# Attention and two expert layers in one kernel: the values' products of two tiles together every second step, x's transposes in front of them, values converted three steps sooner

## The chip, the cores and the metric

One core of a Trainium2 chip runs one launch. The time is device microseconds; the median of three runs of the kernel before is 1000.96 us (998.5 to 1001.49). The profiled execution, from which every duration below comes, took 1003.76 us, of which 1002.0 us lie between the first and the last instruction.

## The reference

Three stages follow each other. The first is causal attention with a position bias for 4 batches, 8 heads, 576 positions and 64 columns per head:

```
s_pos = maximum(s, 0);  cum = cumsum(s_pos, -1)
scores = q @ k.T / 8 + minimum(-(cum_i - cum_j), 0), causal
attn = exp(scores - max) / (sum + 1e-9)
x = (attn @ v), heads side by side: [2304, 512]
```

The second is `relu(x @ w_in)**2 @ w_out` (512 to 2048 to 512), the third `g = h * cos(h)` with `h = x @ w_in`, then `g @ w_out`, with weights of its own. Everything is float32.

## The kernel before

Precision comes from splitting a number into a high and a low part and adding three products (high*high, low*high, high*low). The first expert layer does this in a 32-bit type for TensorE (`F32R`), attention's values and the second expert layer in float16.

The 2304 tokens form nine blocks of 256. Attention's work is cut into 160 jobs: a job is one head (of one of 12 stretches of queries) times one tile of up to 128 queries. The 32 jobs of the first 16 heads (`EARLY`) are computed from float32 values, the other 128 ("late") from split float16 values. A job passes through a pipeline, one stage per step of the main loop, and `step` (called for every step) writes the instructions of all engines in its order: scores (`emit_qk`, line 496, TensorE, into one of three PSUM buffers), mask and row maximum (`emit_mask`, line 510, VectorE), exponentials (`emit_exp`, line 527, ScalarE), the split into two float16 parts and the transposition of both by a DMA on SyncE's queue (`emit_split`, lines 555 to 565, from tile `p` to tile `pt`, three buffers), and the products with the values (`emit_pv`, line 590, TensorE, 3 products for every 128 keys, 64 columns each, into `pvs`). Job j's products stand at the end of step j+5 (`LAG`). When the two heads of a pair are through (every four jobs where heads have two tiles, every two where they have one), `evacuate` (lines 618 to 630, VectorE) divides by the sums in the next step and writes `xp`; `turn` (line 644, TensorE) transposes it through the identity into `xps` at the end of that step, after the products; `x_high` and `x_low` (lines 655, 661) split it in the step behind.

Between these stand the products of the first expert layer for the block that attention has finished: `g1` (line 844, 12 products, called G1 below) and `g2` (line 873, 12 products, G2). A step has one to two such slots: first slot, scores, second slot, the values' products, transposes.

The values are prepared in 16 groups of two heads, on a list `vq` from which every step takes one entry at its end (`v_late`): load (GpSimd queue, line 379), squares (`v_square`, ScalarE, line 390), their sum over partitions by a product with ones (`v_sum`, line 398, TensorE, into another part of `xps`), a power of two from it (`v_scale`, VectorE, lines 404 and 409), high and low part, and the store to `v_d`, from which `load_v` reads per head. `v_steps` puts the groups on steps: `V_TIME` says how long before its first use a group is due.

After the last attention block the second expert layer (lines 1230, 1285) runs from about 620 us to the end.

Of the kernel before, what the change touches and what calls it, by code (L numbers as in the profile page):

```python
# [8 lines left out]
F32 = mybir.dt.float32  # L9
# [81 lines left out]

KQ = 832

WAHEAD = 8
# [15 lines left out]
V_NEAR = 6  # L110
V_TIME = 7


@with_exitstack
def attention_moe_moe_kernel(
# [44 lines left out]

    ones = const.tile([128, 128], F32, name="ones")
    yss = const.tile([128, 2 * NB1], F32, name="yss")
# [41 lines left out]
    def load_sums(x, eng):  # L204
        nc_ = c8[2 * x:2 * x + 2, 0:BT]
        eng.dma_start(out=early[x][64:65, :, BT:2 * BT], in_=nc_)
        eng.dma_start(out=early[x][65:66, :, 0:BT], in_=nc_)

    def load_raw(n):
        nq, nl = heads[n][6], heads[n][8]  # L210
        if n < H:
            return
        if n < EARLY:
            t = at.tile([128, KQ], F32, tag=("hi", "k2")[n % 2], bufs=2, name="early1")
            nc.sync.dma_start(out=t[0:64, 0:2 * BT], in_=qk[n, 0:64, 0:2 * BT])
            nc.sync.dma_start(out=t[64:66, 0:2 * BT], in_=c1_d[n - H])
            hd[n] = t
            return
        raw = at.tile([128, KQ], F32, tag="raw", bufs=2, name="raw")
        nc.sync.dma_start(out=raw[:, BT - nq:BT + nl], in_=qk[n, :, BT - nq:BT + nl])  # L220
        hd[n] = [None, None, raw]
# [111 lines left out]
    def load_ext(n):  # L333
        nq, nl = heads[n][6], heads[n][8]
        if n < EARLY:
            return
        hd[n][0] = at.tile([128, KQ], F32R, tag="hi", bufs=2, name="hi")
        hd[n][1] = at.tile([128, KQ], F32R, tag="k2", bufs=2, name="k2")
        nc.gpsimd.dma_start(out=hd[n][1][64:68, BT - nq:BT + nl], in_=ext_d[n, :, BT - nq:BT + nl])  # L339

    def prep_high(n):
        nq, nk = heads[n][6], heads[n][8]
        if n < EARLY:
            return
        hi, k2, raw = hd[n]
        nc.scalar.copy(hi[:, BT - nq:BT + nk], raw[:, BT - nq:BT + nk])
        nc.scalar.copy(k2[0:64, BT - nq:BT], raw[0:64, BT - nq:BT])

    def prep_low(n):
        nq, nk = heads[n][6], heads[n][8]  # L350
        if n < EARLY:
            return
        hi, k2, raw = hd[n]
        nc.vector.tensor_tensor(
            out=hi[64:128, BT - nq:BT], in0=raw[64:128, BT - nq:BT], in1=hi[64:128, BT - nq:BT], op=ALU.subtract
        )
        nc.vector.tensor_tensor(  # L357
            out=k2[0:64, BT:BT + nk], in0=raw[0:64, BT:BT + nk], in1=hi[0:64, BT:BT + nk], op=ALU.subtract
        )
# [35 lines left out]
    def v_sum(g):  # L395
        n = g[2]
        vs[g]["ps"] = xps[:, BT:BT + n]
        nc.tensor.matmul(vs[g]["ps"], ones, vs[g]["ss"])

# [48 lines left out]
    def v_steps(gs, start):  # L448

        at, due = [], len(jobs) + V_TIME  # L450
        for b, h, n, nch in reversed(gs):
            first = next(
                i for i, j in enumerate(jobs) if j[0] >= 2 * H and heads[j[0]][1] == b and h <= heads[j[0]][2] < h + n
            )
            due = min(first - start + 3 - V_TIME, due - V_NEAR)
            at.insert(0, due)
        free = 0
        for x, due in enumerate(at):
            at[x] = max(0, min(due, free))
            free = at[x] + V_STRIDE  # L460
        return at

    def v_add(gs, at, stored=True):

        for g, t in zip(gs, at):
            fs = []
            if g not in vs:
                fs, t = [(t, v_load)], t + 2
            fs += [(t, v_square), (t + 1, v_sum), (t + 2, v_scale), (t + 2, v_high), (t + 3, v_low)]
            for x, f in fs + [(t + 3, v_store)] * stored:  # L470
                vq.extend([] for _ in range(x + 1 - len(vq)))
                vq[x].append((f, g))
# [3 lines left out]
    def emit_qk(i):  # L476
# [5 lines left out]
        segs = [(0, 288), (288, 288)] if w > 512 else [(0, max(w, 256))]  # L482
        qo = BT - nq + q - q0
        if n < EARLY:
# [7 lines left out]
        for k, (c0, cn) in enumerate(segs):  # L492
            p = psa.tile([128, 512], F32, tag=f"qk{flip[0]}", bufs=1, name="qkp")
            flip[0] = (flip[0] + 1) % 3
            for m, kk in ((hi, 128), (k2, 68)):
                nc.tensor.matmul(  # L496
                    p[0:r, 0:cn], m[0:kk, qo:qo + r], m[0:kk, BT + c0:BT + c0 + cn],
                    start=(kk == 128), stop=(kk == 68),
                )
# [40 lines left out]
    def emit_split(i):  # L540
# [21 lines left out]
        )  # L562
        pt = at.tile([128, 1280], F16, tag="pt", bufs=3, name="pt")
        pt = pt[:, 0:2 * cw // 128 * r].rearrange("p (a r) -> p a r", r=r)
# [112 lines left out]
    def lag(i):  # L677
        return LAG[not job(i) or jobs[i][0] >= EARLY]

# [5 lines left out]
    def unit_done(u):  # L685
        return last_job[u] + lag(last_job[u]) + 3

# [295 lines left out]
    def step(moe=0, bits=0, attn=True):  # L983

        i = prog[0]
        prog[0] += attn
        if attn:
            for j in stage(1, i - 2):
# [32 lines left out]
        if attn:  # L1021
            for j in stage(0, i - 2):
                if jobs[j][1] == 0:
                    load_v(jobs[j][0])
            for j in stage(3, i - LAG[0]):
                if j > i - lag(j):
                    stages[3] -= 1
                    break
                emit_pv(j)
        turn()  # L1030
        w_ahead()
# [375 lines left out]
```

## Time and profile before

| | before |
|---|---|
| median of 3 runs | 1000.96 us |
| profiled execution | 1003.76 us |
| its span | 1002.0 us |
| TensorE busy in the span | 966.9 us (96%) |
| VectorE busy | 723.9 us (72%) |
| ScalarE busy | 655.5 us (65%) |
| mean granted TensorE clock | 0.995 |

TensorE's matmuls are pipelined, so what a group costs is read from the start of its first to the start of what follows, not from the lengths of the rows. In a window's row the columns after the stretch are the busy time of PE (matmuls), PEld (weight loads), VectorE, ScalarE and GpSimd with the number of instructions, then the granted clock, the DMA engines' share and GB/s. In a timeline row the columns are start, length, engine, line, operation, written tile `<-` read tiles, shape, count, and in brackets the idle time before and what ended it.

### The profile page before, as it was taken

The page shows a single profiled execution, that of the slowest core. Times are in us where ns is not written, and L with a number is a line of the kernel's source. Part 1 is how long each engine was busy: PE and PEld are TensorE (multiplying, and loading weights), DVE is VectorE, ACT ScalarE, POOL GpSimd, SP SyncE. Part 2 cuts the span into 40 slices and gives each one's busy share as a digit, 9 for nine tenths or more (in the row PEclk, how much of TensorE's full clock was granted, in tenths as well). Part 3 has the DMA queues.
Part 4 walks back from the last instruction along what each step waited for, and adds up shares of the span by engine and source line. Part 5 has one row for each costly group of instructions (what it writes and reads, how often), then busy time and mean ns, then how long its engine had stood idle before and what let it go on. Part 6 is the DMA issues. An engine that isn't in the chain of part 4 may idle for free.

```text
span 1002.0 us, 20487 instructions
## 1 busy us (share of the span) xinstructions
PE 966.9 (96%) x7266; PEld 740.6 (74%) x7266; DVE 723.9 (72%) x1865; ACT 655.5 (65%) x1596; POOL 163.2 (16%) x258
## 2 busy tenths in 40 slices
PE   5999899999999999999999999999999999999998
PEld 4788898899999998999999997444544454444444
DVE  6879788867777897787888267798887545555555
ACT  4789777767777777767776578777766444433433
POOL 2000011111111121111211023330033341000000
PEclk9999999999999999999999999999999999999999
DMA  8955599746887986467898569210000000011001
GB/s 268 292 182 181 118 202 203 170 111 157 196 162 160 178 193 175 109 155 145 192 206 180 188 237 360 95 43 1 1 1 1 0 1 1 0 43 43 23 20 64
DMA packets 150711, 126.65 MB, mean 126 GB/s; under 512 B 108048, under 2 KB 125792, under 8 KB 150608
## 3 DMA queue, kind: packets, MB, share of 16 engines
q1 hardware_dynamic: 146688, 119.05, 46.1%
q0 software_dynamic: 3904, 6.29, 2.5%
q8 instruction: 57, 0.93, 0.4%
q14 instruction: 46, 0.38, 0.1%
q10 hardware_dynamic: 16, 0.01, 0.0%
HBM read 85.25 MB, written 15.81 MB: 101 GB/s over the span
## 4 chain that ended last, share of the span: by engine, by line
PE 79%; DVE 8%; DMA 6%; ACT 4%; issue 2%; SPq 1%; DVEq 0%; ACTq 0%
PE hps L844 18%; PE y L873 18%; PE o L1285 17%; PE hp L1230 17%; PE qkp L496 4%; PE pvs L590 4%; DMA rw<-in_w_dram 3%; DMA raw<-in_qk_dram 1%; PE xps L644 1%; DVE st L716 1%; DVE sb L510 1%; DVE gl L863 1%; DVE wt L737 0%; DVE k L357 0%; SPq L178 0%
## 5 line engine op out<-in xcount | busy, mean ns | idle before, releaser
L844 PE MATMUL hps<-xh,wt 128*128 128x256 f32 x1152 | 241.4, 292 | 4.1 <-ACT g L855 4.0
L873 PE MATMUL y<-gh,wt 128*128 128x256 f32 x1152 | 237.7, 289 | 0.0
L844 PEld LDWEIGHTS hps<-xh,wt 128*128 128x128 f32 x1152 | 191.7, 194 | 7.0 <-ACT g L855 5.5
L873 PEld LDWEIGHTS y<-gh,wt 128*128 128x128 f32 x1152 | 189.9, 192 | 1.3
L1230 PE MATMUL hp<-yh,wt 128*128 128x512 f16 (+1 forms) x640 | 185.9, 358 | 0.0
L1285 PE MATMUL o<-wt,gh 128*128 128x512 f16 x576 | 171.3, 379 | 2.0 <-ACT wt L1300 1.9
L873 PE MATMUL y<-gl,wt 128*128 128x256 f32 x576 | 163.4, 284 | 2.6 <-DVE gl L863 2.6
L844 PE MATMUL hps<-xl,wt 128*128 128x256 f32 x576 | 164.3, 285 | 0.9 <-DVE xl L661 0.9
L1230 PEld LDWEIGHTS <-wt 128*128 128x128 f16 x960 | 92.2, 98 | 93.3
L1242 ACT ACTIVATE a<-hp,hsc 128x512 f32<-128x512 f32 (+1 forms) x80 | 51.4, 643 | 118.6 <-PE hp L1230 117.2
L855 ACT ACTIVATE g<-hps 128x256 f32<-128x256 f32 x144 | 54.6, 379 | 107.7 <-PE hps L844 105.8
L1230 PE MATMUL hp<-yl,wt 128*128 128x512 f16 (+1 forms) x320 | 114.4, 358 | 0.0
L873 PEld LDWEIGHTS y<-gl,wt 128*128 128x128 f32 x576 | 110.6, 192 | 3.7 <-DVE gl L863 3.1
L844 PEld LDWEIGHTS hps<-xl,wt 128*128 128x128 f32 x576 | 111.7, 194 | 1.4 <-DVE xl L661 1.1
L1285 PE MATMUL o<-wt,gl 128*128 128x512 f16 x288 | 109.2, 379 | 0.4 <-DVE gl L1272 0.4
L1243 DVE TENSOR_SCALAR kf<-a 128x512 f32<-128x512 f32 (+1 forms) x80 | 34.5, 431 | 103.8 <-ACT a L1242 103.4
L1285 PEld LDWEIGHTS <-gh 128*128 128x128 f16 x576 | 56.2, 98 | 66.7 <-issue 2.4
L527 ACT ACTIVATE sb<-sb,nb 128x128 f32<-128x128 f32 (+8 forms) x160 | 93.7, 586 | 12.1 <-DVE nb L510 12.0
L339 POOL DMA_DIRECT2D k<-ext_d x80 | 40.8, 510 | 341.9 <-ACT g L856 92.3
L510 DVE CUSTOM_DVE_ANT_0 sb<-qkp,mask 128x128 f32<-128x128 f32 (+8 forms) x160 | 72.7, 454 | 13.8 <-PE qkp L487 8.6
L1251 ACT ACTIVATE a<-kf 128x512 f32<-128x512 f32 (+1 forms) x80 | 46.8, 585 | 46.6 <-DVE kf L1244 46.1
L559 DVE SCALAR_TENSOR_TENSOR p<-sb,p 128x512 f16<-128x512 f32 (+7 forms) x128 | 72.4, 565 | 4.0
(119 smaller groups left out, 1680.1 us busy)
## 6 DMA issues: line engine op xcount, KB each, us to landing
rw<-in_w_dram SPq DMA_DIRECT2D x64, 512.0 KB
raw<-in_qk_dram SPq DMA_DIRECT2D x32, 352.0 KB
raw<-in_qk_dram SPq DMA_DIRECT2D x16, 384.0 KB
v_d<-vt SPq DMA_DIRECT2D x16, 320.0 KB
raw<-in_qk_dram SPq DMA_DIRECT2D x16, 320.0 KB
vb<-v_d SPq DMA_DIRECT2D x32, 160.0 KB
vr<-in_v_dram POOLq DMA_DIRECT2D x15, 320.0 KB, 4.7
y_d<-yst SPq DMA_DIRECT2D x18, 256.0 KB
```

Source lines behind the costliest of these rows:

```text
L339: nc.gpsimd.dma_start(out=hd[n][1][64:68, BT - nq:BT + nl], in_=ext_d[n, :, BT - nq:BT + nl])
L496: nc.tensor.matmul(p[0:r, 0:cn], m[0:kk, qo:qo + r], m[0:kk, BT + c0:BT + c0 + cn], start=(kk == 128), stop=(kk == 68),)
L510: nc.vector.tensor_tensor_reduce(out=sb[0:r, c0:c0 + cn], in0=p[0:r, 0:cn], in1=mask[0:r, mo + c0:mo + c0 + cn], scale=-0.125, scalar=(3.0 ...
L527: nc.scalar.activation(out=sb[0:r, 0:w], in_=sb[0:r, 0:w], func=ACTF.Exp, scale=-1.0, bias=j["nb"], accum_out=pd[n - h % 2]["z"][0:r, ti, ...
L559: nc.vector.scalar_tensor_tensor(out=p[0:r, cw:cw + w], in0=sb[0:r, 0:w], scalar=PSC, in1=p[0:r, 0:w], op0=ALU.mult, op1=ALU.subtract,)
L844: nc.tensor.matmul(hp, w[:, a, c * 128:(c + 1) * 128], (xh, xl)[e][:, c, :], start=(n == 0), stop=(n == 3 * KD - 1),)
L855: nc.scalar.activation(out=g, in_=hp, func=ACTF.Relu)
L873: nc.tensor.matmul(yps[k][d // 2][:, d % 2, :], w[:, a, d * 128:(d + 1) * 128], (gh, gl)[e], start=(f == 0 and n == 0 and d % 2 == 0), sto ...
L1230: nc.tensor.matmul(hp, w[:, a, c * 128:(c + 1) * 128], (yh, yl)[e][:, c, :], start=(m == 0), stop=(m == 3 * KD - 1),)
L1242: nc.scalar.activation(out=a, in_=hp, func=ACTF.Copy, scale=sm["hsc"][:, j, f:f + 1], bias=0.25)
L1251: nc.scalar.activation(out=a, in_=kf, func=ACTF.Sin, scale=-6.2831850)
L1285: nc.tensor.matmul(ops[j][a], (gh, gl)[e][:, a * 128:(a + 1) * 128], w[:, x, :], start=(first and m == 0), stop=(last and m == 2),)
```

## The change

Late jobs of odd number have a lag of 4 steps instead of 5, so that jobs 2m and 2m+1 both have their products at the end of step 2m+5, and the steps between have none. In a step with late products `turn` is called in front of them; in a step without, it is held back to the next. `pt` gets a fourth buffer for every fourth job (`pt4`, or `vt`'s space where the tile is largest); the space comes from narrower rows (`SQ` 768 instead of 832, with the place of the queries' start computed by `qb`) and from a `ones` of one column that is read as if it were 128. The groups of values start on even entries of `vq`, `V_TIME` is 10 instead of 7, and the sum comes two entries after the squares instead of one, with what follows one entry later too.

```diff
@@ -90,6 +90,7 @@
 KQ = 832
+SQ = 768
-V_TIME = 7
+V_TIME = 10
...
-    ones = const.tile([128, 128], F32, name="ones")
+    ones = const.tile([128, 1], F32, name="ones")
...
+    def qb(n):
+        return min(BT, SQ - heads[n][8])
...
-        raw = at.tile([128, KQ], F32, tag="raw", bufs=2, name="raw")
-        nc.sync.dma_start(out=raw[:, BT - nq:BT + nl], in_=qk[n, :, BT - nq:BT + nl])
+        raw = at.tile([128, SQ], F32, tag="raw", bufs=2, name="raw")
+        nc.sync.dma_start(out=raw[:, qb(n) - nq:qb(n) + nl], in_=qk[n, :, BT - nq:BT + nl])
...
-        nc.tensor.matmul(vs[g]["ps"], ones, vs[g]["ss"])
+        nc.tensor.matmul(vs[g]["ps"], ones.to_broadcast([128, 128]), vs[g]["ss"])
...
-            at[x] = max(0, min(due, free))
+            at[x] = max(0, min(due, free)) // 2 * 2
...
-            fs += [(t, v_square), (t + 1, v_sum), (t + 2, v_scale), (t + 2, v_high), (t + 3, v_low)]
-            for x, f in fs + [(t + 3, v_store)] * stored:
+            fs += [(t, v_square), (t + 2, v_sum), (t + 3, v_scale), (t + 3, v_high), (t + 4, v_low)]
+            for x, f in fs + [(t + 4, v_store)] * stored:
...
-        pt = at.tile([128, 1280], F16, tag="pt", bufs=3, name="pt")
+        if i % 4 < 3:
+            pt = at.tile([128, 1280], F16, tag="pt", bufs=3, name="pt")
+        elif cw * r <= 512 * 128:
+            pt = at.tile([128, 1024], F16, tag="pt4", bufs=1, name="pt4")
+        else:
+            pt = at.tile([128, 1280], F16, tag="vt", bufs=1, name="pt5")
...
     def lag(i):
-        return LAG[not job(i) or jobs[i][0] >= EARLY]
+        if job(i) and jobs[i][0] < EARLY:
+            return LAG[0]
+        return LAG[1] - (i % 2 if job(i) else 0)
...
-        return last_job[u] + lag(last_job[u]) + 3
+        return last_job[u] + lag(last_job[u]) + (4 if u > 1 else 3)
...
+        hold = False
...
+            js = []
             for j in stage(3, i - LAG[0]):
                 if j > i - lag(j):
                     stages[3] -= 1
                     break
+                js.append(j)
+            if js and jobs[js[0]][0] >= EARLY:
+                turn()
+            for j in js:
                 emit_pv(j)
-        turn()
+            if not js and job(i - 4) and jobs[i - 4][0] >= EARLY:
+                hold = True
+        if not hold:
+            turn()
```

Three places in the order of the instructions show what moves. On TensorE, in the third block (tiles of 128 and 64 queries), the kernel before has the products of the second tile (64x64), a G1, the scores of the next pair, the first tile's products and the transposes of the pair that went before, then a G2:

```order
L873 MATMUL y_2910<-gh,wt 128x256
L590 LDWEIGHTS pt
L590 MATMUL pvs<-vb,pt 64x64
...
L844 MATMUL hps<-xh,wt 128x256
...
L496 MATMUL qkp<-hi 128x448
L496 MATMUL qkp<-k_3489 128x448
L590 LDWEIGHTS pt
L590 MATMUL pvs<-vb,pt 128x64
...
L644 MATMUL xps<-ident,xp 128x128
L644 MATMUL xps<-ident,xp 128x64
L873 MATMUL y_2909<-gh,wt 128x256
```

The same place with the change, where lines 855 and 884 are G1 and G2, 500 the scores, 653 the transposes, 599 the values' products and 402 the sum with ones:

```order
L855 MATMUL hps<-xh,wt 128x256
L500 MATMUL qkp<-hi 128x448
L500 MATMUL qkp<-k_3497 128x448
L653 MATMUL xps<-ident,xp 128x128
L653 MATMUL xps<-ident,xp 128x64
L599 LDWEIGHTS pt
L599 MATMUL pvs<-vb,pt 128x64
...
L599 LDWEIGHTS pt
L599 MATMUL pvs<-vb,pt 64x64
...
L402 MATMUL xps<-ss,ones 128x2
L884 MATMUL y_2935<-gh,wt 128x256
```

The transposes stand between the scores and the products, both tiles' products (3 and 6 here) stand together, and one of the sums stands behind them; between G1 and the scores there are no products any more.

On VectorE, around the same pair's evacuation (z is the tile of the sums, `sb` the masked scores, `p` the split), before:

```order
L357 TENSOR_TENSOR k2_3568<-raw_3431,hi_3567 64x448
L618 SCALAR_TENSOR_TENSOR z_3228<-z_3228,vsc_89 128x2
...
L630 SCALAR_TENSOR_TENSOR xp_3638<-pvs_78,z_3228 128x128
L630 SCALAR_TENSOR_TENSOR xp_3638<-pvs_78,z_3228 64x128
L510 ISA sb_3645,nb_3646<-qkp_3600,mask_86 128x320
...
L555 TENSOR_SCALAR p_3648<-sb_3584 64x192
```

and with the change (line 639 evacuates, 514 masks, 559 splits):

```order
L874 TENSOR_TENSOR gl_3560<-g_3524,gh_3525 128x256
L627 SCALAR_TENSOR_TENSOR z_3248<-z_3248,vsc_89 128x2
...
L639 SCALAR_TENSOR_TENSOR xp_3596<-pvs_78,z_3248 128x128
L639 SCALAR_TENSOR_TENSOR xp_3596<-pvs_78,z_3248 64x128
L514 ISA sb_3603,nb_3604<-qkp_3562,mask_86 64x192
...
L514 ISA sb_3651,nb_3652<-qkp_3619,mask_86 128x320
```

The evacuation stands one job sooner: in front of the mask of a pair's last tile (64x192) instead of the mask of the next pair's first (128x320).

On TensorE the sum with ones (line 398, with the change 402) stood behind products or transposes in every late group; before, in the second block:

```order
L496 MATMUL qkp<-k_1450 128x512
L590 LDWEIGHTS pt
L590 MATMUL pvs<-vb,pt 128x64
...
L873 MATMUL y_1627<-gh,wt 128x256
L873 MATMUL y_1627<-gl,wt 128x256
```

and the sum of that block with the change:

```order
L855 MATMUL hps<-xl,wt 128x256
L855 MATMUL hps<-xh,wt 128x256
L402 MATMUL xps<-ss,ones 128x2
L884 MATMUL y_1644<-gh,wt 128x256
L884 MATMUL y_1644<-gl,wt 128x256
```

Seven of the late groups' sums stand like this one, alone between G1, G2 or scores; the others stand behind products or transposes.

## Rows read from the trace of the kernel before

**Rows 1.** Windows: four stretches, columns as told above.

```profile
110.00:200.00 90.00, 82.91 (x785) 77.29 (x786) 74.39 (x210) 65.43 (x179) 12.87 (x28) 0.96 0.81 178
200.00:480.00 280.00, 278.65 (x2713) 265.54 (x2711) 214.14 (x687) 206.52 (x581) 41.93 (x112) 1.00 0.71 159
480.00:560.00 80.00, 78.03 (x851) 76.48 (x850) 64.35 (x187) 53.87 (x138) 10.02 (x30) 1.00 0.81 176
620.00:1002.00 382.00, 375.24 (x1853) 178.72 (x1851) 247.00 (x453) 198.84 (x370) 75.95 (x58) 1.00 0.08 29
```

**Rows 2.** Timeline of TensorE, one step of the fourth block.

```profile
300.46 0.29 PE L844 MATMUL hps<-xh,wt 128*128 128x256 f32 x1
...
301.90 0.43 PE L590 MATMUL pvs<-vb,pt 128*128 128x64 f16 x9
302.17 0.36 PE L873 MATMUL y<-gh,wt 128*128 128x256 f32 x1
...
303.69 0.34 PE L496 MATMUL qkp<-hi 128*128 128x384 f32 x1
```

**Rows 3.** The same around transposes of x behind products.

```profile
309.52 0.42 PE L644 MATMUL xps<-ident,xp 128*128 128x128 f32 x2
309.69 0.36 PE L873 MATMUL y<-gh,wt 128*128 128x256 f32 x1
309.89 0.28 PE L873 MATMUL y<-gl,wt 128*128 128x256 f32 x1
```

**Rows 4.** The same where transposes stood behind a G1.

```profile
109.97 0.44 PE L644 MATMUL xps<-ident,xp 128*128 128x128 f32 x2 [0.38 <-DVE xp L630]
110.17 0.36 PE L873 MATMUL y<-gh,wt 128*128 128x256 f32 x1
```

**Rows 5.** Transpositions by DMA: line 565's instructions, nanoseconds least, median, most.

```profile
L565 SPq DMA_TRANSPOSE pt<-p x128: 1167/1225/2385, 107.1 to 549.6; - x128
```

**Rows 6.** Waits of TensorE from 110 to 560 us: total, times, longest.

```profile
PE hps L844 <- ACT g L855: 3.2, 4, 1.4
PE pvs L590 <- DVE xp L630: 2.5, 2, 1.4
PE xps L398 <- ACT vt L390: 1.5, 1, 1.5
```

**Rows 7.** Timeline: the two longest of these waits, and VectorE before the second.

```profile
117.74 0.38 PE L398 MATMUL xps<-ss,ones 128*128 128x2 f32 x2 [1.55 <-ACT vt L390]
...
194.25 0.68 DVE L881 COPY yst<-y 128x512 f32<-128x512 f32 x1
195.22 0.28 DVE L630 SCALAR_TENSOR_TENSOR xp<-pvs,z 64x128 f32<-64x128 f32 x1
...
195.55 0.63 PE L590 MATMUL pvs<-vb,pt 128*64 128x64 f16 x15 [1.39 <-DVE xp L630]
```

**Rows 8.** Windows: two stretches at half clock.

```profile
118.10:121.50 3.40, 3.40 (x16) 3.21 (x16) 1.22 (x4) 0.66 (x2) 0.00 (x0) 0.50 0.10 38
196.60:200.00 3.40, 3.40 (x18) 3.40 (x18) 2.53 (x11) 1.70 (x6) 0.37 (x1) 0.51 1.49 303
```

**Rows 9.** Timeline of TensorE around a sum with ones.

```profile
204.35 0.38 PE L398 MATMUL xps<-ss,ones 128*128 128x2 f32 x2
204.59 0.36 PE L873 MATMUL y<-gh,wt 128*128 128x256 f32 x1
```

**Rows 10.** Waits of SyncE's queue from 110 to 560 us.

```profile
SPq L565 <- PE pvs L590: 81.5, 71, 3.9
```

**Rows 11.** Timeline: transpositions' issues, and fillings of `p` that waited for one.

```profile
193.24 1.33 SPq L565 DMA_TRANSPOSE pt<-p  x1
...
197.62 0.37 POOL L554 MEMSET p<- 64x128 f16 x1 [2.44 <-DMA pt<-p]
...
535.65 1.34 SPq L565 DMA_TRANSPOSE pt<-p  x1
...
540.00 0.21 POOL L554 MEMSET p<- 128x128 f16 x1 [4.63 <-DMA pt<-p]
```

**Rows 12.** Timeline: a split's end, and the products two steps on.

```profile
435.38 0.62 DVE L559 SCALAR_TENSOR_TENSOR p<-sb,p 128x448 f16<-128x448 f32 x1
...
440.77 0.44 PE L590 MATMUL pvs<-vb,pt 128*128 128x64 f16 x9
```

**Rows 13.** The page's DMA issues: KB each, median us to landing.

```profile
vr<-in_v_dram POOLq DMA_DIRECT2D x15, 320.0 KB, 4.7
```

More of the change, by code (lines that the diff above doesn't have):

```diff
@@ L213, in load_raw @@
         if n < EARLY:
-            t = at.tile([128, KQ], F32, tag=("hi", "k2")[n % 2], bufs=2, name="early1")
+            t = at.tile([128, SQ], F32, tag=("hi", "k2")[n % 2], bufs=2, name="early1")
             nc.sync.dma_start(out=t[0:64, 0:2 * BT], in_=qk[n, 0:64, 0:2 * BT])
@@ L336, in load_ext @@
             return
-        hd[n][0] = at.tile([128, KQ], F32R, tag="hi", bufs=2, name="hi")
-        hd[n][1] = at.tile([128, KQ], F32R, tag="k2", bufs=2, name="k2")
-        nc.gpsimd.dma_start(out=hd[n][1][64:68, BT - nq:BT + nl], in_=ext_d[n, :, BT - nq:BT + nl])
+        hd[n][0] = at.tile([128, SQ], F32R, tag="hi", bufs=2, name="hi")
+        hd[n][1] = at.tile([128, SQ], F32R, tag="k2", bufs=2, name="k2")
+        nc.gpsimd.dma_start(out=hd[n][1][64:68, qb(n) - nq:qb(n) + nl], in_=ext_d[n, :, BT - nq:BT + nl])
     def prep_high(n):
@@ L345, in prep_high @@
         hi, k2, raw = hd[n]
-        nc.scalar.copy(hi[:, BT - nq:BT + nk], raw[:, BT - nq:BT + nk])
-        nc.scalar.copy(k2[0:64, BT - nq:BT], raw[0:64, BT - nq:BT])
+        nc.scalar.copy(hi[:, qb(n) - nq:qb(n) + nk], raw[:, qb(n) - nq:qb(n) + nk])
+        nc.scalar.copy(k2[0:64, qb(n) - nq:qb(n)], raw[0:64, qb(n) - nq:qb(n)])
     def prep_low(n):
@@ L354, in prep_low @@
         nc.vector.tensor_tensor(
-            out=hi[64:128, BT - nq:BT], in0=raw[64:128, BT - nq:BT], in1=hi[64:128, BT - nq:BT], op=ALU.subtract
+            out=hi[64:128, qb(n) - nq:qb(n)], in0=raw[64:128, qb(n) - nq:qb(n)], in1=hi[64:128, qb(n) - nq:qb(n)], op=ALU.subtract
         )
         nc.vector.tensor_tensor(
-            out=k2[0:64, BT:BT + nk], in0=raw[0:64, BT:BT + nk], in1=hi[0:64, BT:BT + nk], op=ALU.subtract
+            out=k2[0:64, qb(n):qb(n) + nk], in0=raw[0:64, qb(n):qb(n) + nk], in1=hi[0:64, qb(n):qb(n) + nk], op=ALU.subtract
         )
@@ L482, in emit_qk @@
         segs = [(0, 288), (288, 288)] if w > 512 else [(0, max(w, 256))]
-        qo = BT - nq + q - q0
+        qo = qb(n) - nq + q - q0
         if n < EARLY:
@@ L496, in emit_qk @@
                 nc.tensor.matmul(
-                    p[0:r, 0:cn], m[0:kk, qo:qo + r], m[0:kk, BT + c0:BT + c0 + cn],
+                    p[0:r, 0:cn], m[0:kk, qo:qo + r], m[0:kk, qb(n) + c0:qb(n) + c0 + cn],
                     start=(kk == 128), stop=(kk == 68),
```

## The prediction

> **What bounds the kernel now.** I read the windows first. From 200 to 480 us TensorE is busy for 278.7 of 280 us, and from 480 to 560 for 78.0 of 80; from 110 to 200 it misses 7 of 90, and the clock there is 0.96 [rows 1]. VectorE, the next engine, is at 83, 76 and 80% in the three stretches [rows 1]: the largest load beside TensorE, but not the bound. So in the stretch that the change touches, time goes only where TensorE needs less of it: fewer or cheaper instructions, or fewer waits. The timeline of TensorE comes next, for what an instruction costs in its place: the reader is to compare starts, not lengths. Then the waits of TensorE, with the few that are long [rows 6, 7], the clock behind them [rows 8], and last the transpositions, whose latency could make the shorter lag a new wait [rows 10 to 12].
>
> **Products in pairs.** The late jobs are the 128 that have a transposition by DMA [rows 5]; their products now stand in 64 places instead of 128. The products themselves stay. What goes is the change of kind: a G1 without products in front takes from 300.46 to 301.90, 1.44 us; a G2 behind products takes from 302.17 to 303.69, 1.52 us [rows 2]. So 0.08 us per place, and 64 places less: **-5.1 us**. It lies on TensorE, which waits for nothing there, so all of it counts. A change of kind that costs more at tiles of 64 queries would raise it; no row here bounds that, and I leave it out.
>
> **Transposes in front.** Two transposes behind products take from 309.52 to 309.69, 0.17 us, and the G2's first product then still takes 0.20 (to 309.89) [rows 3]. The change of kind back to G1 or G2 is counted above, once per pair of jobs. In front of the products the two cost at least the columns: 256 columns take a twelfth of 1.44 us, 0.12 [rows 2]; the nearest row is two transposes behind a G1 after a short wait, 0.20 us (109.97 to 110.17) [rows 4]. So between 0.05 us less and 0.03 more at each of 40 pairs of heads (80 late heads), -2.0 to +1.2 us; I take the middle, **-0.4**.
> The Trainium skill (TensorE: Matmul & The Clock Gate, LDWEIGHTS) gives a load of stationary values as columns over 1.2 GHz, an estimate of 0.107 us for 128 of them, and lets the next load run beside the present matmul. By that rule the second transpose of a pair waits for its own load wherever the two stand, so the move is worth only what the first one gains, and the sum would be the same within half a microsecond; no run here shows it apart.
>
> **Waits that the new order takes away.** TensorE waited 2.5 us for evacuations in two places [rows 6]: at 195.55 a pair's first products started 0.05 us after the evacuation that stood in the same step in front of them ended (195.22 plus 0.28) [rows 7]. With the change the evacuation stands a job sooner, and the next products a step later than it: a step is G1, products, G2 and scores, 300.46 to 303.69 and the scores, some 3.6 us [rows 2], and the waits were 1.4 us at most [rows 6]. **-2.5.** The one wait for the squares of the values, 1.5 us at 117.74 [rows 6, 7], goes because the sum stands two entries behind the squares instead of one: **-1.5.** About half a microsecond behind the end of each of these two longest waits the granted clock falls to 0.50, the lower of the two levels, for 3.4 us (118.1 and 196.6) [rows 8]; at half speed 3.4 us do the work of 1.7. Without the waits I take both falls as gone, **-3.4**; if waits elsewhere bring them back, 0.
>
> **SyncE's queue.** Transpositions stood at its head for 81.5 us because their buffer was still to be read by products of that step [rows 10]. With four buffers and the products of 4m, 4m+1 at step 4m+5, 4m+2 and 4m+3 at 4m+7, every buffer is read a step before its next writing, so the transposition goes when the split is done, and the loads of values, scores' rows and the first layer's stores behind it go sooner. Of the 3.2 us that TensorE waited for ScalarE's g [rows 6] a part is late rows of this queue: between 0 and -3.2, I take **-0.8**, since the loads' transfers take as long as before.
>
> **What it adds.** Seven late sums with ones stand alone between other products, so each has a change of kind of its own: the sum takes 0.24 us either way (204.35 to 204.59) [rows 9], the change 0.08: **+0.6.** Values: load, squares, sum, parts and store now span six entries and the next group's load stands on the entry of the last group's low part, whose input buffer it overwrites; the load waits on GpSimd for VectorE, with rows of the scores and fillings of `p` behind it. It lands 4.7 us after its issue [rows 13], and the squares come two steps later, 7.2 us in long steps: hidden; in the blocks with 24 jobs for the same 32 slots a step is some 2.7 us, two are 5.4, and a late load holds ScalarE and through it G2. Bounds 0 to +3. Waits that the uneven steps make (3.3 us without products, 3.9 with) are in no row: 0, if VectorE at 76 to 83% follows, and at most as many as stand there now, 4.0 us of the above [rows 6]. For both together I take the half of that, **+2.0.**
>
> **The sum.** -5.1 - 0.4 - 2.5 - 1.5 - 3.4 - 0.8 + 0.6 + 2.0 = -11.1 us. The profiled execution took 1003.76 us (1.76 of it around the span), which gives 992.7; it is 2.8 us above the median of the runs shown, 1000.96. What the second expert layer does behind 620 us is unchanged and starts earlier by the same amount. From the median: **990.0 us**. With the small terms at their ends (falls of the clock stay, +3.4; transposes +1.6 or -1.6; SyncE +0.8 or -2.4; new waits +3.0 or -2.0) added as independent errors, 985 to 995.
>
> **Rivals.**
> *Only the change of kind.* The waits of rows 6 and 7 come back a few steps on, since they come from ScalarE and VectorE being late at the ends of blocks, and the clock falls with them. For it: waits at such places have several causes [rows 6]. Against it: two of them hang on an order that is gone. -5.1 - 0.4 + 0.6 is -4.9: 996.
> *VectorE becomes the bound.* In the stretches at 80 and 83% [rows 1], 170 us long, the steps without products are 0.3 us shorter than the mean, and VectorE has a third of a microsecond less for its share; if TensorE then waits for what it gains there, nothing is left of the gain in 170 of 450 us, and the old waits, which lie there, stay. About two thirds of 4.9 are left: 998. Against it: VectorE's idle time is 17 to 24%, and a backlog of 0.3 us has the next step to be worked off.
> *Slower: the odd tile's products wait for its transposition.* They now come at the end of the second step after the split, where the even ones have three. In the shortest steps a split ends at 436.00, and products stand at 440.77: 4.8 us [rows 12]. Nearly always less is needed: a filling of `p` waited for a transposition issued at 193.24 and began at 197.62, so 4.4 us were enough [rows 11]. From 4.8 us on, each of the 24 pairs in the two blocks of short steps waits for the difference, and everything on TensorE behind it; at 5.3 us the gain of 11 is spent (24 times 0.5 is 12), at 5.6 it is 24 times 0.8, 19 us, and the time is 1009. For it: transpositions now run beside the loads that they used to come after. Against it: 4.4 us was one of the long ones, after a queue of loads, and the transpositions are issued earlier after the split than before.
> *More goes.* If the other waits of 110 to 200 us (7 us of TensorE idle [rows 1]) go too, 982.
>
> **How the numbers follow.** The forecast 0.62, only the change of kind 0.18, VectorE 0.11, slower 0.05, more 0.04. About 0.3%, 3 us, is what a measurement of this kernel can tell from no change. The forecast and "more" are faster; of the change-of-kind case nine tenths; of VectorE's case a third: faster 0.86, the same 0.09, slower 0.05. The range takes the forecast's own 985 to 995, the first rival, and part of the others: 984 to 997.
>
> **What would show it.** Right: 64 groups of products where 128 were; a G1 or G2 behind none of them at 1.44 us; no wait of SyncE's transpositions for products; no wait of products for an evacuation, nor of the sum for squares; no fall of the clock near 118 and 196 us; attention's end, the last transposition by DMA, some 11 us earlier. Wrong: products that wait with no engine named, which would be transpositions; waits for VectorE's masks, gl or splits of more than 4 us together; or a clock at half speed at new places.

## The result: slower, and the profile after

| | before | after |
|---|---|---|
| median of 6 runs | 1001.01 us (998.5 to 1003.16) | 1009.81 us (1008.06 to 1011.76) |
| ratio | | 1.009 [1.007, 1.011] |
| profiled execution | 1003.76 us | 1008.63 us |
| its span | 1002.0 us | 1006.8 us |
| TensorE busy | 966.9 us | 961.2 us |
| mean granted TensorE clock | 0.995 | 0.989 |

The forecast was 990.0 us, so it missed by 20 us and on the wrong side. TensorE is busy 5.7 us less than before, as was meant; it stands idle longer. Line numbers from here on are those of the changed kernel unless a row is of another: 599 is the values' products, 653 the transposes, 855 G1, 884 G2, 500 the scores (491 and 542 are the early heads' scores and transposes), 394, 402, 422 and 429 a value group's squares, sum, high and low part, 436 its store, 383 its load, 563 and 574 split and transposition, 371 the load of a head's values.

The windows of after answer [rows 1]. In 200 to 480 us TensorE is now busy for 272.2 us instead of 278.7, in 110 to 200 for 84.8 instead of 82.9; the clock of the first stretch has risen from 0.96 to 1.00:

```profile
110.00:200.00 90.00, 84.76 (x850) 80.50 (x849) 78.42 (x219) 69.49 (x188) 13.45 (x29) 1.00 0.75 174
200.00:480.00 280.00, 272.15 (x2662) 262.66 (x2663) 211.85 (x689) 204.91 (x581) 40.93 (x109) 0.99 0.71 160
480.00:560.00 80.00, 79.39 (x844) 77.79 (x843) 67.02 (x193) 54.76 (x141) 11.69 (x33) 1.00 0.87 185
```

The waits of TensorE from 110 to 560 us answer [rows 6]. None of the three rows of before is left; one of 4.8 us for a head's values and two groups of waits of the scores stand there instead:

```profile
PE pvs L599 <- DMA vb<-v_d: 4.8, 1, 4.8
PE qkp L500 <- DVE nb L514: 3.3, 5, 1.0
PE qkp L500 <- DVE p L563: 2.8, 2, 1.9
...
PE pvs L599 <- DMA pt<-p: 0.2, 1, 0.2
```

The longest wait behind the kernel's start lies ahead of that stretch, in a part of which the prediction had shown no row. TensorE's timeline there:

```profile
81.12 0.55 PE L592 MATMUL pvs<-vr,pt 128*128 128x64 f32 x4
90.42 0.69 PE L542 MATMUL qkp<-ident,sb 128*128 128x128 f32 x2 [8.75 <-ACT sb L531]
```

**The first stall, 8.75 us at 81.7.** The chain of waits of that stretch (start, length, what) says what ScalarE's `sb` hung on: a store of `vt`, 9.19 us from issue to landing, and behind it the squares of the second value group:

```profile
77.92 0.46 DVE vt L429
...
78.78 9.19 DMA v_d<-vt
...
88.08 1.01 ACT vt L394 x4
```

The load of that group's input (line 383) left GpSimd's queue 0.19 us later than the store was issued, and the squares wait for it as well:

```profile
78.78 0.55 SPq L436 DMA_DIRECT2D v_d<-vt  x1
78.97 0.76 POOL L383 DMA_DIRECT2D vr<-in_v_dram  x1 [72.24 <-ACT st L717]
79.38 1.82 SPq L179 DMA_DIRECT2D rw<-in_w_dram  x2
```

So load, store and squares, meant to be steps apart, meet in one step. The DMA engines were full then (share 0.93 and 1.01 in the rows below), with the weights of the first layer among what they carried (`rw`, line 179). For a DMA that GpSimd issues, as this load, the Trainium skill (DMA: Bandwidth & Descriptors, Anatomy of one DMA) gives some 2.0 us of fixed cost, most of it until the write is confirmed. This load took 7.99 us where it alone was waited for (the run with the squares elsewhere, below), so that the fixed cost is the small part here.

The windows of the clock (the last three columns are granted clock, DMA share, GB/s):

```profile
80.00:84.00 4.00, 1.67 (x15) 1.53 (x14) 0.81 (x2) 0.00 (x0) 0.28 (x1) 1.00 0.93 279
84.00:90.00 6.00, 0.00 (x0) 0.00 (x0) 0.62 (x2) 1.93 (x7) 0.00 (x0) 0.50 1.01 403
...
93.00:94.00 1.00, 1.00 (x6) 0.91 (x5) 1.00 (x3) 1.00 (x5) 0.00 (x0) 0.50 0.00 0
...
95.00:96.00 1.00, 1.00 (x10) 1.00 (x9) 0.57 (x3) 1.00 (x2) 0.00 (x0) 1.00 0.00 0
```

The clock falls from its upper level to the lower one at 84.0, 2.3 us into the wait, and rises again only after 94: TensorE works from 90.4 to about 94.2 at half speed, which costs another 1.9 us.

**The second stall, 4.79 us at 394.7.** The chain of waits there ends in the load of the values of a pair's odd head, 6.29 us from issue to landing, and ahead of it a transposition that SyncE takes over 2.2 us to issue (median of all 128: 1.232):

```profile
390.90 2.23 SPq L574
...
393.18 6.29 DMA vb<-v_d
...
399.51 0.96 PE pvs L599 x15
```

A second wait hides behind this one: TensorE's weight load from the transposed tile could not go before 398.77 either, so values that landed at once would have saved only 0.7 us.

```profile
398.77 0.13 PEld L599 LDWEIGHTS <-pt 128*64 128x64 f16 x1 [4.16 <-DMA pt<-p]
```

What filled the DMA engines, from the timeline of the 2 us ahead:

```profile
388.15 0.53 DVE L429 SCALAR_TENSOR_TENSOR vt<-vr,vsc,vt 128x320 f16<-128x320 f32 x1
388.76 0.37 SPq L436 DMA_DIRECT2D v_d<-vt  x1
389.25 0.39 SPq L224 DMA_DIRECT2D raw<-in_qk_dram  x1
389.27 0.75 POOL L383 DMA_DIRECT2D vr<-in_v_dram  x1 [6.35 <-ACT yj L895]
389.69 0.96 SPq L893 DMA_DIRECT2D y_d<-yst  x2
...
399.51 0.70 PE L599 MATMUL pvs<-vb,pt 128*64 128x64 f16 x10 [4.79 <-DMA vb<-v_d]
```

The next group's load has stood on GpSimd for 6.35 us. The releaser in the brackets is inferred and does not touch that buffer; the low part of line 429, which ends just before, reads what the load overwrites. So it goes half a microsecond behind the store, and both run into a row of scores and the two stores that end a block: 320 + 224 + 320 + 2 x 256 KB, 1.4 MB in some 2 us, with a mean DMA share of 1.0 from 390 to 398. How much of that share is theirs, and how much that of transpositions and other loads, no row shows:

```profile
390.00:392.00 2.00, 2.00 (x20) 2.00 (x19) 1.86 (x8) 1.97 (x9) 0.89 (x4) 1.00 0.99 212
...
394.00:396.00 2.00, 0.72 (x16) 0.55 (x15) 0.68 (x4) 1.11 (x5) 0.51 (x1) 1.00 1.24 306
```

The clock is at half from 398.1 to 404.9; from 399.5 on that costs half of 5.4, 2.7 us:

```profile
399.50:404.90 5.40, 5.39 (x36) 5.32 (x36) 2.80 (x14) 0.55 (x2) 0.20 (x1) 0.50 0.26 70
```

8.75 + 1.9 + 4.8 + 2.7 is 18.2 us of stalls that the kernel before does not have, both where a group of values is loaded and stored.

SyncE's queue answers [rows 10]: waits for products fell from 81.5 to 11.9 us, but those for the split rose from 44.0 to 125.6, in a queue that was to run ahead:

```profile
SPq L574 <- DVE p L563: 125.6, 98, 5.2
...
SPq L574 <- PE pvs L599: 11.9, 11, 2.1
```

TensorE's starts answer [rows 2, 3]. A G1 with nothing in front takes 1.43 us (304.14 to 305.57), a G2 behind products 1.52 (302.28 to 303.80); two transposes in front of products take 0.22 (308.90 to 309.12) where two behind them took 0.17:

```profile
302.28 0.36 PE L884 MATMUL y<-gh,wt 128*128 128x256 f32 x1
...
303.80 0.33 PE L500 MATMUL qkp<-hi 128*128 128x384 f32 x1
...
304.14 0.28 PE L855 MATMUL hps<-xh,wt 128*128 128x256 f32 x1
...
305.57 0.28 PE L884 MATMUL y<-gh,wt 128*128 128x256 f32 x1
...
308.90 0.38 PE L653 MATMUL xps<-ident,xp 128*128 128x128 f32 x2
309.12 0.78 PE L599 MATMUL pvs<-vb,pt 128*128 128x64 f16 x21
```

### The profile page after: what moved, and what is told of

Its sections match the earlier page's. It is cut to its first block, busy times and chain, and to the rows that moved or that the text cites. A ratio compares the mean times of both kernels' runs of the same rounds, so it can differ in the third digit from the quotient of the medians.

```text
span 1006.8 us, 20456 instructions
## 1 busy us (share of the span) xinstructions
PE 961.2 (95%) x7266; PEld 740.1 (74%) x7266; DVE 721.3 (72%) x1865; ACT 654.1 (65%) x1596; POOL 162.6 (16%) x258
## 3 DMA queue, kind: packets, MB, share of 16 engines
q0 software_dynamic: 3904, 6.29, 2.2%
## 4 chain that ended last, share of the span: by engine, by line
PE 76%; DVE 8%; ACT 6%; DMA 5%; issue 4%; SPq 1%; POOL 1%; DVEq 0%; ACTq 0%; POOLq 0%
PE o L1305 17%; PE hps L855 17%; PE hp L1250 17%; PE y L884 16%; PE qkp L500 4%; PE pvs L599 3%; DMA rw<-in_w_dram 1%; DMA v_d<-vt 1%; DMA early<-c_d 1%; DVE sb L514 1%; DVE k L361 1%; ACT sb L531 1%; PE xps L653 1%; DVE gl L874 1%; DMA vb<-v_d 1%
## 5 line engine op out<-in xcount | busy, mean ns | idle before, releaser
L514 DVE CUSTOM_DVE_ANT_0 sb<-qkp,mask 128x128 f32<-128x128 f32 (+8 forms) x160 | 72.5, 453 | 11.9 <-PE qkp L491 5.7
L874 DVE TENSOR_TENSOR gl<-g,gh 128x256 fp32r<-128x256 f32 x144 | 60.0, 417 | 23.6 <-PE y L884 13.8
```

The source lines that it names most:

```text
L514: nc.vector.tensor_tensor_reduce(out=sb[0:r, c0:c0 + cn], in0=p[0:r, 0:cn], in1=mask[0:r, mo + c0:mo + c0 + cn], scale=-0.125, scalar=(3.0 ...
L874: nc.vector.tensor_tensor(out=gl, in0=g, in1=gh, op=ALU.subtract)
```

## The experiments

Ratios are to the kernel before, run on the same chip in the same rounds; 0.001 is 1 us. "Changed kernel" is the one above (1.009).

**Two entries later.** `-V_TIME = 10` / `+V_TIME = 8`. The groups' entries become 0, 6, 12, ... instead of 0, 4, 10, ...

> The changed kernel with V_TIME 8 instead of 10, so that the second group of values has its squares two entries behind the first group's store instead of on the same entry; nothing else differs. Theory A (the store of the first group, through the one buffer vt, holds ScalarE's squares, and TensorE waits 8.75 us for the first layer's scores behind them, at 81.7 us): the store needs 9.2 us to land, two steps there are about 6, so the wait falls to 1 to 3 us, the fall of the clock at 84 us goes with it, and the time falls by 6 to 9.5 us, to 1000 to 1004. The wait for values at 394.7 us (4.8 us) stays. Theory B (the pairs of products make the steps uneven, and VectorE or the transpositions are late wherever the order leaves them the least; the wait at 81.7 is only where it shows): the wait comes back at another place of 60 to 200 us, and the time stays within 2 us of 1009.8.

Measured: 999.64 us, 0.9991 [0.9976, 1.0007]; the wait at 81.7 fell to 2.9 us. Ten microseconds by one number of the values' schedule: theory A. The wait at 394.7, which was to stay, fell to 1.0 without an edit of its own, the first sign that it hangs on the values too. A new wait of 3.1 us stands at 173.7, where scores waited for rows that stood on GpSimd behind a load of values held for 6.76 us.

**A head's values a step sooner.**

```diff
-            for j in stage(0, i - 2):
+            for j in stage(0, i - 1 if job(i - 1) and len(heads[jobs[i - 1][0]][4]) == 1 else i - 2):
```

> The changed kernel, with the values of a head of one tile loaded a step sooner (at the step behind its scores instead of two behind). Theory A (a head of odd number with one tile has its products a step sooner than before but its values no sooner, so one load that stood behind a held transposition and two stores comes too late, 4.8 us at 394.7): that wait goes and with it the fall of the clock at 398, 1.7: 1009.8 - 6.5 = 1003. The wait at 81.7 stays at about 8.75. Theory B (uneven steps): the products at 394.7 then wait for their transposition or for VectorE instead, and the time stays above 1007.

Measured: 1009.07 us, 1.0101 [1.0082, 1.012]: no gain. The same products at the same place now wait for their transposition:

```profile
PE pvs L599 <- DMA pt<-p: 3.1, 1, 3.1
```

Theory A is wrong in its cause of the second stall: it is not the step of the load alone. The transposition was as late in the changed kernel (398.77 above), and the sooner load only changed the name of the wait. The chain of that run has a transposition of 7.05 us:

```profile
393.68 7.05 DMA pt<-p
```

**Both.** The edits of these two runs in one kernel.

> Both edits of the two runs before in one kernel. Theory A: both waits and both falls of the clock go, 8.75 + 4.8 + 2 x 1.7 = 17 us less at most, 13 to 16 since a part of the store's wait stays: 994 to 997, which is 4 to 7 us faster than the kernel before and leaves what the prediction counted on TensorE (64 changes of kind at 0.08 us, the waits for evacuations), less the transposes in front. Theory B: the sum is less than the two parts, and the time stays at 1001 or above.

Measured: 998.7 us, 0.9991 [0.9981, 1.0001]. Against the first run alone nothing is gained; the expected 994 to 997 was too low, and the 1001 of theory B too high.

**The values' part undone**, all else kept (`V_TIME` 7, no rounding, the sum one entry behind the squares).

> The changed kernel with the values' part of the change undone (V_TIME 7, no rounding to even entries, the sum one entry behind the squares), the pairs, the fourth buffer and the transposes in front kept. Theory A: the squares of the second group stand four entries behind the first store as in the kernel before, so the wait of 8.75 us at 81.7 and the fall of the clock at 84 go: 10.4 us less, 999.4; the wait for the squares near 118 us comes back with its fall of the clock (1.5 + 1.7): up to 1002.6. The wait at 394.7 may stay. Theory B: the pairs themselves cost the 9 us, and the time stays at 1006 or above.

Measured: 997.41 us, 0.9972 [0.9959, 0.9985]. Theory A, and below the 999.4 to 1002.6 that it gave. Without the values' part the change is a small gain.

**The values' part alone**, put into the kernel before.

```diff
-V_TIME = 7
+V_TIME = 10
...
-            at[x] = max(0, min(due, free))
+            at[x] = max(0, min(due, free)) // 2 * 2
...
-            fs += [(t, v_square), (t + 1, v_sum), (t + 2, v_scale), (t + 2, v_high), (t + 3, v_low)]
-            for x, f in fs + [(t + 3, v_store)] * stored:
+            fs += [(t, v_square), (t + 2, v_sum), (t + 3, v_scale), (t + 3, v_high), (t + 4, v_low)]
+            for x, f in fs + [(t + 4, v_store)] * stored:
```

> The kernel before with only the values' part of the change (V_TIME 10, even entries, the sum two entries behind the squares); products, buffers and transposes as before. Theory A (the store of the first group holds the second group's squares in the one buffer vt): the same wait of 8 to 9 us at 80 to 90 us and a fall of the clock (1.7) behind it appear without any pair of products; the wait at 118 (1.5) and its fall (1.7) go: 5 to 8 us slower than the kernel before, 1005 to 1008. Theory B (it takes the pairs to make it slow): within 2 us of the kernel before.

Measured: 1014.26 us, 1.0122 [1.0099, 1.0145], more than expected. The wait is there without any pair of products (lines of the kernel before):

```profile
ACT vt L390 <- DMA v_d<-vt: 9.2, 1, 9.2
```

The part costs 12.2 us here and 1.009 - 0.9972, 11.8 us, in the company of the rest. The sums agree, but that is partly luck, for the second stall is not in this run, although the values' load and store and the block's stores stand together in it too:

```profile
397.96 0.75 POOL L379 DMA_DIRECT2D vr<-in_v_dram  x1 [5.05 <-ACT yst L881]
398.36 0.37 SPq L432 DMA_DIRECT2D v_d<-vt  x1
...
399.30 1.00 SPq L882 DMA_DIRECT2D y_d<-yst  x2
```

No products wait for a DMA here from 60 to 560 us, so the second stall needs the pairs, with the odd tile's products a step sooner, as well. In its place the scores wait 3.2 us at 379.06 for rows that went on GpSimd behind a load held for 7.03 us, with a fall of the clock behind it:

```profile
PE qkp L496 <- DMA k<-ext_d: 4.2, 2, 3.2
```

**The second group's squares written elsewhere.**

```diff
+        if g[:2] == (V_ORDER[0], 2):
+            sq = at.tile([128, 1024], F16, tag="pt4", bufs=1, name="sq")[:, 0:nch * D]
...
-                out=st["vt"][:, x, :, 1], in_=st["vr"][:, x], func=ACTF.Square,
+                out=st["vt"][:, x, :, 1] if sq is None else sq, in_=st["vr"][:, x], func=ACTF.Square,
```

> The changed kernel with its entries as they are (V_TIME 10), only the second group's squares write what nobody reads to the space of the fourth pt buffer instead of vt, so that they needn't wait for the first group's store; vt is first written by that group's high part, three entries behind the store. Theory A (it is this one buffer): the wait of 8.75 us at 81.7 falls to at most 2 (three steps of 2 to 3 us against 9.2 for the store, and the input's own landing), the clock's fall at 84 goes: 999 to 1001. A rival within it, C (it isn't the buffer but that three entries sooner everything of the values meets the loads of the weights: the input lands late as well): the squares then wait for their input for 4 us or more, and the time stays above 1004.

Measured: 1008.48 us, 1.0076 [1.0053, 1.0098]. Theory A's form "it is this one buffer" fell: the squares now wait for their input, which left at 79.27, and start 0.8 us sooner than before:

```profile
87.28 0.47 ACT L398 ACTIVATE sq<-vr 128x320 f16<-128x320 f32 x1 [8.04 <-DMA vr<-in_v_dram]
```

The chain of this run leads from the low part to the load and from it to the squares, so it is the low part that the load had stood for:

```profile
77.75 0.94 DVE vt L436 x2
...
79.27 7.99 DMA vr<-in_v_dram
```

The chain had named the later of two waits of nearly equal length; to take that one away showed the other.

**The second group's input elsewhere as well**, into a buffer of `p`'s, so that the load waits for no low part.

```diff
+        if g[:2] == (V_ORDER[0], 2):
+            vr = at.tile([128, 1280], F16, tag="p", bufs=2, name="vr2").bitcast(F32)
```

> The changed kernel with its entries (V_TIME 10), the second group's input loaded to a buffer of p's and its squares written to the fourth pt buffer's space, so that it waits neither for the first group's low part nor for its store. Theory A (81.7 is two single buffers, the input's and vt, which the distance of four entries asks for too soon): the load goes 7 us sooner, the wait of 8.75 falls below 1.5 and the clock's fall at 84 goes, 10 us less; 394.7 stays: 998 to 1001. Theory C (loads at that time are slow because of the weights, whatever their buffers): the input still lands 8 us behind its issue, but that is at 80 us, in front of the squares: the wait still falls, so that only a wait of 4 us or more would speak for something else.

Measured: 1000.06 us, 0.9994 [0.9979, 1.0008], with `V_TIME` and all entries as in the changed kernel. The stall at 81.7 is gone (the early transposes wait 0.7 us at most): it is the two single buffers, `vr` and `vt`, asked for four entries after the first group instead of six or more. The one at 394.7 stands, at 4.8 us behind a load that takes 6.29 us again, with store, load and the first of the block's stores again within a microsecond:

```profile
379.94 0.37 SPq L446 DMA_DIRECT2D v_d<-vt  x1
380.45 0.75 POOL L386 DMA_DIRECT2D vr<-in_v_dram  x1 [6.35 <-ACT yj L905]
380.87 0.97 SPq L903 DMA_DIRECT2D y_d<-yst  x2
```

**The sum one entry behind the squares again**, so that the low part stands an entry in front of the next load.

```diff
-            fs += [(t, v_square), (t + 2, v_sum), (t + 3, v_scale), (t + 3, v_high), (t + 4, v_low)]
-            for x, f in fs + [(t + 4, v_store)] * stored:
+            fs += [(t, v_square), (t + 1, v_sum), (t + 2, v_scale), (t + 2, v_high), (t + 3, v_low)]
+            for x, f in fs + [(t + 3, v_store)] * stored:
```

> The changed kernel with the sum one entry behind the squares again (V_TIME 10 and the even entries kept), so that a group's low part stands one entry in front of the next group's load instead of on the same entry. Theory A (a load that stands on the entry of the low part whose input buffer it overwrites holds GpSimd's queue and the fillings of p behind it, and by them split, transposition and SyncE): GpSimd's waits at line 383, 102 us without the first group's in the changed kernel, fall to about 42 as in the kernel before; the products' wait of 4.8 us at 394.7 goes with its clock fall (6.5), and of the 8.75 at 81.7 about one step, 3, since load, low part and store come a step sooner; the wait of 1.5 at 118 comes back: 1000 to 1003. Theory B (the late stall is the shorter lag's own): 394.7 stays, 1006 or above.

Measured: 1002.11 us, 1.0013 [0.9998, 1.0027]. The first stall fell to 5.8 us, a step, as expected; the second to 2.6 and not to nothing. Store and load of the values (383.86 and 384.11) now stand 5 us ahead of the block's stores (388.79); GpSimd stood 2.29 us at that load instead of 6.35. The expected return of the 1.5 us at 118 came as 0.4. These readings are of the slowest of its twelve executions, 1005.87 us.

**Both:** the input elsewhere and the sum one entry behind.

> The edits of the two runs before in one kernel: V_TIME 10, even entries, other buffers for the second group, the sum one entry behind the squares. Theory A: neither stall is left, and it stands where the old values' schedule stands, 995 to 999 (997.4 there). Theory B (values three steps sooner cost by themselves): above 1002.

Measured: 995.05 us, 0.9945 [0.9923, 0.9966]. With the values' groups on the entries of the changed kernel and neither long stall, the profiled execution has a mean clock of 1.000. Its values go at 375.0 and 375.3, 5 us ahead of the block's stores (379.98), and the odd head waits 1.7 us. Over all twelve kernels with pairs, the products at that place wait 3.1 to 4.8 us in the four where the values' store and load go within a microsecond of the block's stores, and 0 to 2.6 us in the eight where 4.6 us or more lie between the load and these stores. No run moves the block's stores alone, so that this part is read from the traces and not shown by itself. TensorE's longest waits from 60 to 560 us:

```profile
PE qkp L510 <- DVE nb L524: 3.5, 7, 1.3
PE qkp L552 <- ACT sb L541: 3.4, 3, 1.5
PE xps L663 <- DVE vsc L415: 2.2, 3, 0.9
PE pvs L609 <- DMA vb<-v_d: 2.0, 2, 1.7
```

**Transposes behind the products**, in the run with the old values' schedule (the early call of `turn` left out).

> The kernel of the run with the old values' schedule (997.4), with the transposes of x behind the products instead of in front. By the runs of starts in the changed kernel two transposes in front take 0.218 us and 0.171 behind: 40 times 0.047 is 1.9 us less, 995.5. If instead the transposes in front gain what the prediction counted (0.4 us), it is 997.8; if x is then later for G1 of the next block, one wait of up to 1 us at each of nine blocks comes, and it is 1000 or more.

Measured: 997.45 us, 0.9971 [0.9945, 0.9997], against 0.9972 with them in front: no difference, but the intervals leave 3 us either way, so that neither 1.9 us less nor 0.4 more is decided.

**The same with the loads a step sooner.**

> The same with the values of one-tile heads loaded a step sooner as well. Theory A: in the run with the old values 1.6 us of waits for values' loads and up to one fall of the clock (1.7) were left: another 1 to 3 us less than the run before it, 992 to 995. Theory D (a load and the transposition of the same products stand in one queue, SyncE's, and what holds it, holds both, so that sooner loads only change the name of the wait): no difference within 1 us, waits for pt in the place of waits for vb.

Measured: 995.31 us, 0.9941 [0.992, 0.9963]. Better than the run before by 3.0 us in the ratios and 2.1 in the medians, but the intervals overlap: inconclusive between its two theories. In the profiled executions the waits for `vb` (3.0 us in the run before) are gone, and those for `pt` are 4.6 instead of 2.9; this one took 1000.29 us, 5 above the median.

**All remedies**: buffers, sum, transposes behind, loads sooner.

> The same with the transposes of x behind the products and the values of one-tile heads loaded a step sooner, as in the fastest run so far (995.3, 0.994 of the kernel before). By theory A as fast as that one or a little faster, since the values now land sooner: 992 to 996.

Measured: 994.78 us, 0.9939 [0.9919, 0.9958], the fastest of all, not to be told from 995.05. It is faster than both kernels: 6 us than before, 15 than the changed one.

**The pairs undone in that kernel** (`lag` gives every late job 5 steps).

```diff
-        return LAG[1] - (i % 2 if job(i) else 0)
+        return LAG[1]
```

> The kernel of the last run (all remedies, 0.994 of the kernel before) with the pairs undone: every late job has its products at the end of step j+5, so 128 places instead of 64; fourth buffer, values' schedule and sooner loads stay. If the change of kind is worth 0.08 us at each of 64 places, as the prediction counted and the starts in the changed kernel show, it is 5.1 us slower less what small waits the uneven steps cost: 997 to 1000, ratio to the kernel before 0.997 to 1.000. If the pairs' gain is eaten by waits they bring (transpositions late for the odd tile, 4.5 us in five places in the last run; masks, 3.7 us), it is within 1.5 us of the last run: ratio 0.993 to 0.996.

Measured: 1001.53 us, 1.0005 [0.9991, 1.0018]. The pairs are worth 1.0005 - 0.9939, 6.6 us (give or take 2.4, from the two intervals). What comes back without them are evacuation waits (the row of [rows 6] in another kernel):

```profile
PE pvs L609 <- DVE xp L649: 3.0, 3, 1.7
```

That profile is of an execution of 1010.48 us, 9 above the median of its 13, so the row shows where waits return and not what they cost in most executions.

## Why the prediction was wrong

**The step that failed: the values' term under "What it adds", called "hidden" and put at "0 to +3" within the +2.0.** The prediction named the place: the next group's load "stands on the entry of the last group's low part, whose input buffer it overwrites", with fillings of `p` behind it on GpSimd. It then priced a load "4.7 us after its issue" against squares "two steps later". Both numbers are of a load that goes at its entry. This one can't: it goes when the low part has ended. For the first two groups, four entries apart, the low part, the store and the second group's squares stand on the same entry, so nothing of the 7.2 us was left, and the load and the store took 8.0 and 9.2 us beside the weights, where the prediction had 4.7 for the load. At 394.7 the same late load joined the store and the block's own stores, which the prediction did not look for: it priced each transfer alone. The place was right and "0 to +3" mis-sized: the values' part measures 12 us. With other buffers for the second group and the sum an entry sooner nothing of it is left on the same entries (0.9945). Beside it stood up to 4.0 for uneven steps, and half of the 4.0 alone was taken for both terms, so that the range had no room for it either. The distance of 4 entries against a group's length of 6 could be read from the schedule's own rule.

**The second error: waits of one execution were taken for the kernel's.** The profiled execution of before had a clock of 0.995 and three falls of some 3.4 us each: the two of [rows 8], and one from 56 to 60 us that the prediction did not look at and the changed kernel has too:

```profile
56.00:60.00 4.00, 3.86 (x20) 3.86 (x21) 2.07 (x9) 3.74 (x9) 0.00 (x0) 0.59 0.97 281
```

Of 82 other runs of before with their clocks, the 21 at 1.000 have a median of 999.1 us and the 22 at 0.996 or less one of 1002.8. The median clock is 0.998, which by an estimate (0.002 of 1000 us, at half speed) leaves room for 4 us at the lower level, one such fall. So two falls (-3.4), taken from the median time, are more than a typical run has to give.

With the pairs undone and the fourth buffer, sooner values and sooner loads kept, the time is 1.0005: the fourth buffer and what it was to free on SyncE's queue (-0.8) gain nothing that can be told from no change. That run also undoes the sooner evacuations (-2.5) and has the sum one entry behind the squares, so it does not test those terms, and how the 6.6 us divide between change of kind and evacuations is not shown. "Only the change of kind", the first rival, with -4.9, is near what the change is worth once the values' stalls are out: -2.8 with the old values' schedule (0.9972), -5.5 and -6.1 with the remedies (0.9945 and 0.9939).

Point by point: **change of kind (-5.1)**: right, starts of 1.43 and 1.52, and 6.6 by undoing it (part of which may be the evacuation waits). **Transposes in front (-0.4)**: wrong sign in the rows, 0.22 us against 0.17, 40 times 0.05 is +1.9, a little beyond the bound; the run with them behind can't tell it from nothing. By the Trainium skill's rule (TensorE: Matmul & The Clock Gate, LDWEIGHTS) two transposes, each behind a load of its own, are an estimate of 0.21 us; the trace agrees in front of the products, and not behind them. **Evacuations and sum**: their waits went from the profile, as said; what that is worth in a typical run is not shown. **Falls of the clock**: those at 118 and 196 went, two longer ones came, at 84 and 398. **SyncE (-0.8)**: the waits for products went to 11.9, not to nothing, and the queue waits for splits instead; ScalarE's g, 3.2 us of TensorE's waiting, does not show any more from 110 to 560 us. **Lone sums (+0.6)**: in the order on TensorE seven stand alone against one before (117.74), so six more instead of seven; no run measures their price. **The slower rival** (odd tile's transposition) shows as a wait of 0.2 us, but it hides behind the wait for values at 394.7, and comes out as 2 to 5 us in all where the loads are sooner. It was not spread over the 24 pairs that the rival priced. **VectorE** did not become the bound: the scores' waits for masks and splits are 6.1 us, somewhat above the 4 that were to show it, and stay at 3.5 in the run at 0.9945. Of the signs named as wrong two came, the half-speed clock at new places and, narrowly, these 6.1 us. The last transposition by DMA stands at 554.1 us instead of 549.6, where it was to come 11 us earlier.

## What to carry to other kernels

When a schedule is moved sooner, lay the buffer's last reader, the load that overwrites it and that load's reader on one line of steps, for the first groups apart from the regular ones: in this kernel a load that stood on that reader's entry, or ahead of it, had no head start, and went together with the store that follows the same reader. A wait that the profile names may hide a second of the same length, so take both away before a cause is believed. And before a wait or a fall of the clock from one profiled execution is booked as a gain, compare that execution's time and clock with the other runs of the same kernel.

## What the runs showed that was not expected

A store and a load of 320 KB, issued 0.2 us apart while the weights filled the DMA engines, took 9.2 and 8.0 us (the load's in the run in which it alone was waited for, 0.1 us behind the store there), where the median for that load is 4.7 us [rows 13]. The clock at its lower level lasted on for 3.8 us after TensorE had work again behind the first stall and 5.4 behind the second, against 3.4 in [rows 8], so that each of these stalls cost its length and 2 to 3 us.
